# Clustered attention and a two-of-eight expert layer on one core: v's scales on ScalarE, stores and third list later, other staging for pairs 13 and 14

## The chip, the core and the metric

The kernel runs as one launch on one core of a Trainium2 chip. The metric is the device time in microseconds (us), lower is better. TensorE (PE; PEld is its weight load), VectorE (DVE), ScalarE (ACT) and GpSimd (POOL) compute, and SyncE (SP) issues most DMAs. Each engine works through its own queue in the order in which the kernel's text issued the instructions; between engines only semaphores count.

## The reference

Attention over 4 batches, 8 heads, 768 positions, head size 64; a query sees only keys whose nearest centroid (of 16) is its own. Its output, 3072 rows of 512, goes through an expert layer in which each row uses its two best of 8 experts.

```python
mask = q_assign[:, :, :, None] == k_assign[:, :, None, :]
scores = np.where(mask, scale * q @ k.T, -1e9)
x = softmax(scores) @ v                       # 3072 rows of 512
noisy = x @ w_gate + log1p(exp(x @ w_noise)) * noise
top2 = argpartition(-noisy, 2)[:, :2];  w = softmax(noisy[top2])
out[rows of e] += w * (relu(x @ w1[e]) @ w2[e])     # e = 0 .. 7
```

## The kernel before

**Attention.** Heads go in 16 pairs (4 pairs a batch). The loop over steps `t` runs 12 steps a pair: each step makes the scores of one head's 128 keys against 768 queries (`scores`, line 531), their exponential on ScalarE (line 532, tile `pe`), the lower half of that exponential (`split_p`, line 543, tile `pl`: the f32 value less its upper 16 bits) and, four steps later, the products with v (`values`, lines 560 to 566). The lower halves run on GpSimd up to step 173, and on VectorE from step 174 (pair 14's sixth block) on.

Everything else is hung into this loop by a table `sched`: `at(step, f, ...)` puts a call into one of three slots of a step (thirds). `w = 12 * (p - 2)` is a pair's base, `z` is `w + 40` of a batch's last pair, or 192 in the lines behind the loop over pairs. The number is only a place in the text, not a time: an engine does its instructions in that order, as soon as what they wait for is there. Of the calls that matter here:

- `x_am` (line 611), once for each half batch: four numbers a partition, v's scales times the batch's power of two (`px`), a `tensor_scalar` on VectorE, at step 48b+7.
- `x_hi` (ACT, line 629), `x_lo` (GpSimd, line 633) and `x_put` (a DMA on SP, line 639): a pair's output as two f16 halves, stored to `xs` in DRAM. A pair goes in two pieces, i = 0 and 1. Pairs 1 to 12 use one tile `xh`, and one store. Pairs 13 and 14 use two tiles each of the pool `xg`, which has four buffers and which the gathers of the experts use too. Pair 15 is done after the attention.
- `a_mask`, `b_mask`: a pair's cluster mask, built and put by four DMAs (tile `mk`) into the operand `A`, 3.3 steps ahead of its maxima (`b_max`).
- `g_gate`, `g_list`: batch by batch the gate is computed on VectorE, and each row's place and weight are scattered into the table `tbl` by 12 indirect DMAs on GpSimd (line 821), each behind a small memset (line 820). The third batch's gate ends in a part that starts with `places` (matmuls, line 733). Batch 3 has no scatter: its list is made by matmuls inside the expert part.
- `load_w1`, `load_w2`: the first expert's weights, eight loads of 512 KB into the tile `stg` (seven buffers); `max_w1`, `max_w2` and `split_w1`, `split_w2` take their largest value and their two f16 halves.
- `load_list(0)` (line 840) reads the first expert's first four columns of the table once all 36 scatters have landed; `gather_x(0, t)`, t = 0 to 3 (lines 1172, 1173), clears an `xg` tile on GpSimd and gathers 128 rows of `xs` into it.

**Experts.** `turn_x` turns a gathered tile by a transposing DMA on SP (line 1184); `layer1` (line 1193) needs all four for its first block, and the halves of w1 from `split_w1`. `layer1` of expert 0 interleaves with batch 3's gate. From `layer2(0, 0)` on (line 1230), expert follows expert.

Of the kernel before, what the change touches and what calls it, by code (L numbers as in the profile page):

```python
# [9 lines left out]
F32 = mybir.dt.float32  # L10
F32R = mybir.dt.float32r
BF = mybir.dt.bfloat16
F16 = mybir.dt.float16
I32 = mybir.dt.int32
AF = mybir.ActivationFunctionType
OP = mybir.AluOpType
# [28 lines left out]
class Kernel:  # L45
# [136 lines left out]
    def attention(self, ctx):  # L182
        nc, tc = self.nc, self.tc
        B, H, S, D, NJ = self.B, self.H, self.S, self.D, self.NJ
# [9 lines left out]
        NP = B * H // 2  # L194
# [6 lines left out]
        def at(step, f, *a):  # L201
            sched.setdefault(divmod(round(3 * step), 3), []).append((f, a))

        def chain(step, by, fs):
            for i, f in enumerate(fs):
                at(step + by * i, f)


        T = AT
        for p in range(NP):  # L210
            b, hp = divmod(p, H // 2)
            w = 12 * (p - 2)
            if hp == 0:
                for g in range(2):
                    at(w + T["qk"] + 24 * g + (T["qf"] if (b, g) == (0, 1) else 0), self.load_qk, b, g)
                    v = w + 24 * g
                    V = T["fv"][g] if p == 0 else T
                    at(v + V["v"], self.load_v, b, g)
                    for h in range(0, 4, 2):
                        at(v + V["vscale"] + V["amstep"] * h, self.v_max, b, g, h)  # L220
                    chain(v + V["am"], V["amstep"], self.v_scale(b, g))
                    for h in range(4):
                        at(v + V["vsplit"] + V["vstep"] * h, self.v_split, b, g, h)
            if p == 0:
                at(17.333, self.x_first)
            for i in range(2):
                if p == 0:
                    hi, lo = 18.667 + 1.333 * i, 20.0 + 1.333 * i
                elif p <= NP - 4:
                    hi, lo = w + 34.667 + 6 * i, w + 36 + 6 * i  # L230
                else:
                    hi, lo = w + 40.667 + 0.333 * i, w + 41.333 + 0.333 * i
                if p < NP - 1:
                    at(hi, self.x_hi, p, i)
                    at(lo, self.x_lo, p, i)
                    if p > NP - 4 or i:
                        at(lo + 1, self.x_put, p, i)
            P = T["first"] if p == 0 else T
            w += (0, T["sec"], T["thr"])[p] if p < 3 else 0
            for i in range(4):  # L240
                at(w + P["split"][i], self.a_split, p, i // 2, i % 2)
            if p == 0:
                at(w + P["sims"][0], self.c_turn)
            at(w + P["place"] + (T["place1"] if p == 1 else 0), self.b_place, p)
            for s in range(2):
                at(w + P["sims"][s], self.a_sims, p, s)
            for s in range(2):
                at(w + P["sum"][s], self.a_sum, p, s)
            for k, f in (("max1", self.a_max1), ("ge", self.a_ge), ("ky", self.a_ky), ("max2", self.a_max2),
                         ("eq", self.a_eq), ("mask", self.a_mask), ("bmask", self.b_mask)):  # L250
                at(w + P[k], f, p)
            if p == 0:
                for s in range(2):
                    for j in range(NJ):
                        at(w + P["bmax"][s] + P["bstep"][s] * j, self.b_max, p, s, j)
                    at(w + P["neg"][s], self.b_neg, p, s, 1)
                    at(w + P["negT"][s], self.b_negT, p, s, 1)
            else:
                w = 12 * (p - 2)
                bm, bs = (T["bmax1"], T["bstep1"]) if p == 1 else (T["bmax"], T["bstep"])  # L260
                for s in range(2):
                    for j in range(NJ):
                        at(w + bm + bs * (6 * s + j), self.b_max, p, s, j)
                at(w + T["neg"], self.b_neg, p, 0, 2)
                at(w + T["negT"], self.b_negT, p, 0, 2)
            if hp == H // 2 - 1:
                z = w + 36 + L
                if b + 1 == B:
                    continue
                for jj in range(NJ):  # L270
                    at(z + T["log"] + T["logstep"] * jj, self.g_logits, b, jj)
                    at(z + T["log2"] + T["logstep"] * jj, self.g_logits2, b, jj)
                at(z + T["turn"], self.g_turn, b)
                fs = self.g_gate(b)
                k = b == B - 2
                chain(z + T["gate"], T["gstep"] / (1 + k), fs[:self.GP])
                chain(z + (12.333 if k else T["gplace"]), T["gstep"] / (1 + k), fs[self.GP:])
                for j in range(2 * NJ):
                    at(z + (15.333 + 2 * min(j, 5) + max(j - 5, 0) if k else T["list"] + T["lstep"][b] * j), self.g_list, b, j)
        at(T["zlist"], self.zero_list)  # L280
        at(-13, self.exp_table)
        at(10.667, self.load_gate)
# [2 lines left out]
        z = 12 * NP  # L285
# [8 lines left out]
        for i in range(4):  # L294
            at(z - 24 + i, self.load_w1, 0, i)
            at(z - 13 + 2 * i, self.max_w1, 0, i)
            at(z - 4 + 2 * i, self.split_w1, 0, i)
            at(z - 8 + i if i < 3 else z - 2, self.load_w2, 0, i)
        at(z - 11.667, self.load_list, 0)
        for i in range(self.TA):  # L300
            at(z - 5.333 + 0.333 * i, self.gather_x, 0, i)
        for i in range(2):
            nc.gpsimd.memset(self.oh[i], 0.0)
        nc.gpsimd.memset(self.nm.bitcast(F32), 0.0)
# [4 lines left out]
        for t in range(min(sched)[0], z + L + 2):  # L309
# [8 lines left out]
            if 0 <= u < z:  # L318
                p, s, kc = u // 12, (u % 12) // 6, u % 6
# [288 lines left out]

    def x_am(self, b, g):
        am = self.am[b, g]  # L610
        self.nc.vector.tensor_scalar(am[:, 0, :], am[:, 2, :], self.px[:, b:b + 1], None, op0=OP.mult)

    def x_piece(self, p, i):
        b, c = divmod(p, self.H // 2)
        if p <= self.NP - 4:
            cs = slice(64 * i, 64 * i + 64)
            return self.xt[b][:, :, 128 * c + 64 * i:128 * c + 64 * i + 64], self.xh[:, :, 0, cs], self.xh[:, :, 1, cs]
        return self.xt[b][:, 3 * i:3 * i + 3, 128 * c:128 * c + 128], self.xh[i][:, :, 0], self.xh[i][:, :, 1]

    def x_hi(self, p, i):  # L620
        NJ = self.NJ
        if p > self.NP - 4:
            pool, n, k = (self.mo, "xh", 2) if p == self.NP - 1 else (self.mw, "xg", 4)
            t = pool.tile([128, 2 * self.DM], F16, name=n, bufs=k)
            self.xh = (self.xh if i else []) + [t[:, :NJ * 128].rearrange("p (j i c) -> p j i c", i=2, c=128)]
        elif i == 0:
            self.xh = self.pre.tile([128, NJ, 2, 128], F16, name="xh")
        x, hi, lo = self.x_piece(p, i)
        self.nc.scalar.activation(hi, x, AF.Copy)
# [5 lines left out]
    def x_put(self, p, i):  # L635
        b, c = divmod(p, self.H // 2)
        NJ, W = self.NJ, 2 * self.DM
        j, n, h = (3 * i, 3, self.xh[i]) if p > self.NP - 4 else (0, NJ, self.xh)
        self.nc.sync.dma_start(rap(self.xs, (b * 128 * NJ + j) * W + 256 * c, [[NJ * W, 128], [W, n], [1, 256]]),
                               h.rearrange("p j i c -> p j (i c)"))  # L640

# [213 lines left out]
    def experts(self, ctx):  # L855
        nc, tc, E, DM, F, N, CAP, T, TA = self.nc, self.tc, self.E, self.DM, self.F, self.N, self.CAP, self.T, self.TA
        ND, NF, NJ, b = DM // 128, F // 128, self.NJ, self.B - 1
# [10 lines left out]
        Bs = (TA * 128, CAP)  # L868
        for t in range(TA):
            self.turn_x(0, t)  # L870
        self.load_list(1)
        for c in range(4):
            self.max_w2(0, c)
        self.layer1(0, 0, [A])
        for j in range(NJ):
            self.g_logits(b, j)
            if j:
                self.g_logits2(b, j - 1)
        self.g_logits2(b, NJ - 1)
        for f in (self.x_hi, self.x_lo, self.x_put):  # L880
            for i in range(2):
                f(self.NP - 1, i)
        self.g_turn(b)
        fs = self.g_gate(b)
        cut = [0] + AT["cut"] + [self.GP, len(fs)]
# [277 lines left out]
    def split_w2(self, e, c):  # L1163
        self.scaled_halves(self.w2t[:, :, 2 * c:2 * c + 2], self.stg[2, c], self.sw2)

    def gather_x(self, e, t):
        xg = self.mw.tile([128, 2 * self.DM], F16, name="xg", bufs=4)
        r = self.rows(t)
        first = e == 0 and t < self.TA
        n = self.N - self.S if first else self.N  # L1170
        if first:
            self.nc.gpsimd.memset(xg, 0.0)
        self.nc.gpsimd.indirect_dma_start(  # L1173
            out=xg[:r], out_offset=None, in_=self.xs[:n],
            in_offset=bass.IndirectOffsetOnAxis(ap=self.entry(e, t)[:r], axis=0),
            bounds_check=n - 1, oob_is_err=False)
        self.xg[e, t] = xg
# [113 lines left out]
```

## Time and profile before

| | |
|---|---|
| time, median of 3 runs | 1084.91 us (1084.48 to 1087.84) |
| profiled execution: time, span | 1085.09 us, 1083.3 us |
| busy in the span: PE, DVE, POOL, ACT | 1008.4, 684.4, 577.5, 513.5 us |
| chain that ended last, by engine | PE 65%, POOL 11%, issue 9%, DVE 8%, DMA 3%, ACT 2% |
| attention's last product ends, first `layer1` starts | 499.3 us, 504.7 us |

The time lies 1.8 us above the span. A busy share over the whole span mixes the attention (to 500 us), where four engines work side by side, with the experts, where PE is busy throughout. So the stretches are read one by one; steps and us are related by about 2.3 us a step, 1.7 us in steps 163 to 173.

### The profile page before, as it was taken

The numbers are of one execution on the slowest core, as the hardware profiler recorded it, in microseconds if no ns is written. First come the engines' busy times: TensorE is split into PE (matmuls) and PEld (weight loads), VectorE is DVE, ScalarE is ACT, GpSimd is POOL, SyncE is SP. The second block draws the span as 40 slices with busy tenths as digits, with TensorE's granted clock in tenths as the row PEclk, the third lists the DMA queues.
The fourth block names the chain that finished last, engine by engine and source line by source line (L and its number), as shares of the span: only waits on it lengthen the run. The fifth ranks groups of instructions, "written<-read, shape, count | busy, mean of one in ns | idle before, by whom it ended". The sixth has DMA issues, their size and how long they took to land.

```text
span 1083.3 us, 22212 instructions
## 1 busy us (share of the span) xinstructions
PE 1008.4 (93%) x8518; PEld 686.4 (63%) x8518; DVE 684.4 (63%) x1451; ACT 513.5 (47%) x1067; POOL 577.5 (53%) x630
## 2 busy tenths in 40 slices
PE   5789999999899999986999999999999999999994
PEld 4678898889788887874455545545455454554542
DVE  5788677887778777896736644456544555455511
ACT  2467676768676767654513523316233152331510
POOL 9167685789877896872243525225252252432211
PEclk8799999999999999998999999999999999999997
DMA  7676766676757754325088853928739278292200
GB/s 195 166 186 148 179 166 173 160 189 160 189 140 175 178 129 107 122 90 100 15 219 172 218 160 102 226 90 186 180 95 240 86 167 199 89 234 84 59 33 33
DMA packets 154113, 158.09 MB, mean 146 GB/s; under 512 B 68970, under 2 KB 132842, under 8 KB 154003
## 3 DMA queue, kind: packets, MB, share of 16 engines
q1 hardware_dynamic: 140706, 120.25, 46.0%
q0 software_dynamic: 13296, 36.38, 11.9%
q8 instruction: 68, 1.11, 0.4%
q14 instruction: 43, 0.34, 0.1%
HBM read 78.21 MB, written 26.51 MB: 97 GB/s over the span
## 4 chain that ended last, share of the span: by engine, by line
PE 65%; POOL 11%; issue 9%; DVE 8%; DMA 3%; ACT 2%; SPq 0%; POOLq 0%; DVEq 0%; ACTq 0%
PE ring L1193 21%; PE ring L1230 20%; PE ring L531 7%; POOL pl L543 4%; PE ring L500 4%; PE av L560 2%; PE av L566 2%; PE av L562 2%; DVE aux L503 1%; DMA A<-mk 1%; PE ring L398 1%; POOL tbl L821 1%; PE ring L419 1%; PE ring L434 1%; ACT pe L532 1%
## 5 line engine op out<-in xcount | busy, mean ns | idle before, releaser
L543 POOL TENSOR_TENSOR pl<-pe 128x768 f16<-128x768 f32 x173 | 251.7, 1469 | 65.9 <-ACT pe L532 61.8
L1193 PE MATMUL ring<-xT,w1t 128*128 128x416 f16 (+2 forms) x1536 | 275.3, 341 | 5.8 <-DMA xT<-xg 5.8
L1230 PE MATMUL ring<-w2t,hT 128*128 128x512 f16 x1152 | 251.8, 379 | 0.0
L532 ACT ACTIVATE pe<-ring,l 128x384 f32<-128x384 f32 x384 | 201.2, 578 | 65.7 <-PE ring L531 60.1
L1193 PEld LDWEIGHTS <-w1t 128*128 128x128 f16 x1536 | 149.9, 98 | 125.5 <-DMA xT<-xg 6.2
L1077 ACT ACTIVATE hr<-ring 128x416 f32<-128x416 f32 (+2 forms) x128 | 66.7, 521 | 289.3 <-PE ring L1193 289.3
L1230 PEld LDWEIGHTS <-hT 128*128 128x128 f16 x1152 | 112.3, 98 | 133.1
L1243 POOL DMA_INDIRECT out<-yo,idx x52 | 62.6, 1204 | 227.7 <-DVE yo L1239 113.6
L503 DVE TENSOR_REDUCE aux<-ring 128x1 f32<-128x384 f32 x192 | 107.9, 562 | 75.3 <-PE ring L500 70.9
L531 PE MATMUL ring<-A 128*128 128x384 f32 x384 | 143.0, 372 | 1.7 <-DVE aux L503 1.0
L531 PE MATMUL ring<-B 128*128 128x384 f32 x384 | 131.3, 342 | 1.6 <-DMA B<-nt 1.6
L500 PE MATMUL ring<-A 128*128 128x384 f32 x384 | 110.6, 364 | 14.6 <-DMA A<-mk 6.2
L1080 DVE TENSOR_TENSOR hT<-hr,hT 128x416 f16<-128x416 f32 (+3 forms) x128 | 71.2, 559 | 82.0 <-ACT hT L1079 81.7
L1239 DVE SCALAR_TENSOR_TENSOR yo<-ring,we,xt 128x512 f32<-128x512 f32 (+1 forms) x49 | 36.7, 749 | 123.4 <-PE ring L1230 104.0
L503 DVE TENSOR_REDUCE mm<-ring 128x1 f32<-128x384 f32 x192 | 104.9, 547 | 0.0
L1173 POOL DMA_INDIRECT xg<-xs,idx x52 | 56.0, 1077 | 80.8 <-DMA xT<-xg 69.5
L560 PE MATMUL av<-vv,pe 128*128 128x65 f16 x1152 | 97.5, 195 | 1.4 <-DVE xt L574 1.4
L562 PE MATMUL av<-vv,pe 128*128 128x64 f16 x1152 | 96.5, 192 | 0.0
L560 PEld LDWEIGHTS <-pe 128*128 128x128 bf16 x1152 | 79.7, 99 | 16.7 <-issue 11.9
L500 PEld LDWEIGHTS ring<-A 128*128 128x128 f32 x384 | 71.0, 195 | 27.4 <-ACT pe L532 12.1
L562 PEld LDWEIGHTS <-pe 128*128 128x128 bf16 x1152 | 78.1, 98 | 0.3
L531 PEld LDWEIGHTS ring<-A 128*128 128x128 f32 x384 | 74.0, 193 | 3.0 <-DVE aux L503 1.2
(210 smaller groups left out, 1437.9 us busy)
## 6 DMA issues: line engine op xcount, KB each, us to landing
stg<-in_moe_w SPq DMA_DIRECT2D x64, 512.0 KB
A<-hl SPq DMA_DIRECT2D x30, 384.0 KB
B<-hl SPq DMA_DIRECT2D x30, 384.0 KB
vt<-in_v SPq DMA_DIRECT2D x8, 768.0 KB
out<-zt SPq DMA_DIRECT2D x12, 512.0 KB
A<-hl SPq DMA_DIRECT2D x60, 96.0 KB
B<-hl SPq DMA_DIRECT2D x30, 192.0 KB
qk<-in_q SPq DMA_DIRECT2D x7, 768.0 KB
```

The costliest lines, as they stand in the source:

```text
L500: nc.tensor.matmul(t, A[:, 0, s, j * 128:j * 128 + 128], A[:, 1, s, n * 384:n * 384 + 384], start=True, stop=True)
L503: nc.vector.tensor_reduce(o, t, axis=X, op=OP.max, negate=True)
L531: nc.tensor.matmul(t, M[:, 1 - qi, s, ks], M[:, qi, s, ns], start=not qi, stop=bool(qi))
L532: nc.scalar.activation(pe[:, n], t, AF.Exp, bias=self.l64[:, 0:1], scale=self.scale)
L543: (nc.vector if last else nc.gpsimd).tensor_tensor(lo, pe, hi, op=OP.subtract)
L560: nc.tensor.matmul(av[:, j, :], ph[:, js], vv[:, hh, kj, 64:129], start=(kc == 0 and j == 0), stop=False, skip_group_check=True)
L562: nc.tensor.matmul(av[:, j, :64], ph[:, js], vv[:, hh, kj, 0:64], start=False, stop=False, skip_group_check=True)
L1077: nc.scalar.activation(r[:, :n], p, AF.Relu, scale=2.0 ** -HT)
L1080: nc.vector.tensor_tensor(h1, r[:, a:b], h0, op=OP.subtract)
L1193: nc.tensor.matmul(p, self.w1t[:, wi, c, f * 128:f * 128 + 128], self.xT[e][:, c, xi, n0:n1], start=(i == 0), stop=(i == 3 * ND - 1))
L1230: nc.tensor.matmul(p, self.hT[:, hi, f, t * 128:t * 128 + 128], self.w2t[:, wi, f], start=(i == 0), stop=(i == 3 * NF - 1))
L1243: i = nc.gpsimd.indirect_dma_start(out=self.out, out_offset=bass.IndirectOffsetOnAxis(ap=en[:r], axis=0), in_=yo[:r], in_offset=None, boun ...
```

## The change

The products for v's scales go from VectorE to ScalarE. The first piece of x's halves of pairs 1 to 12 is split 3.3 steps later, and the store's call stands at `w + 45` in place of `w + 43`. The end of the third batch's gate starts 1.33 steps later; of its twelve scatters three stand at steps 165.3, 167.7 and 170 (before: six at 163.3 to 173.3, two steps apart, then one a step), the rest at 173 to 175.7. Pair 13's halves use a tile of `stg` and one store; pair 14's two tiles are taken at step 180.67 (`x_tiles`). The clearing of a gather's tile is a call of its own (`clear_x`); tiles 0 and 1 are cleared at steps 181 and 182 and gathered at 182.67 and 183, ahead of pair 14's halves (184.67 to 186.67), tiles 2 and 3 behind its stores. The last two loads of w2 stand behind the four `turn_x`, and their maxima behind pair 15's stores.

```diff
                 elif p <= NP - 4:
-                    hi, lo = w + 34.667 + 6 * i, w + 36 + 6 * i
+                    hi, lo = w + 38 + 2.667 * i, w + 39.333 + 2.667 * i
...
-                    if p > NP - 4 or i:
-                        at(lo + 1, self.x_put, p, i)
+                    if p == NP - 2 or i:
+                        at(w + 45 if 0 < p <= NP - 4 else lo + 1, self.x_put, p, i)
...
-                chain(z + (12.333 if k else T["gplace"]), T["gstep"] / (1 + k), fs[self.GP:])
+                chain(z + (13.667 if k else T["gplace"]), T["gstep"] / (1 + k), fs[self.GP:])
                 for j in range(2 * NJ):
-                    at(z + (15.333 + 2 * min(j, 5) + max(j - 5, 0) if k else ...), self.g_list, b, j)
+                    at(z + ((17.333 + 2.333 * j if j < 3 else 24 + 0.333 * j) if k else ...), self.g_list, b, j)
...
-            at(z - 8 + i if i < 3 else z - 2, self.load_w2, 0, i)
+            if i < 2:
+                at(z - 8 + i, self.load_w2, 0, i)
         at(z - 11.667, self.load_list, 0)
+        at(z - 11.333, self.x_tiles, NP - 2)
         for i in range(self.TA):
-            at(z - 5.333 + 0.333 * i, self.gather_x, 0, i)
+            at(z - 11 + i if i < 2 else z - 6 + 0.333 * i, self.clear_x, i)
+            at(z - 9.333 + 0.333 * i if i < 2 else z - 5.667 + 0.333 * i, self.gather_x, 0, i)
...
     def x_am(self, b, g):
         am = self.am[b, g]
-        self.nc.vector.tensor_scalar(am[:, 0, :], am[:, 2, :], self.px[:, b:b + 1], None, op0=OP.mult)
+        self.nc.scalar.activation(am[:, 0, :], am[:, 2, :], AF.Copy, scale=self.px[:, b:b + 1])
...
+    def x_tiles(self, p):
+        pool, n, k = (self.mo, "xh", 2) if p == self.NP - 1 else (self.mw, "xg", 4)
+        self.xh = [pool.tile([128, 2 * self.DM], F16, name=n, bufs=k)[:, :self.NJ * 128].rearrange(...) for i in range(2)]
...
     def x_hi(self, p, i):
-        if p > self.NP - 4:
-            pool, n, k = (self.mo, "xh", 2) if p == self.NP - 1 else (self.mw, "xg", 4)
-            t = pool.tile([128, 2 * self.DM], F16, name=n, bufs=k)
-            self.xh = (self.xh if i else []) + [...]
-        elif i == 0:
+        if p == self.NP - 3 and i == 0:
+            t = self.mw.tile([128, self.F], F32, name="stg", bufs=7)
+            self.xh = t[:, :NJ * 128].bitcast(F16).rearrange("p (j i c) -> p j i c", i=2, c=128)
+        elif p < self.NP - 3 and i == 0:
             self.xh = self.pre.tile([128, NJ, 2, 128], F16, name="xh")
...
         for t in range(TA):
             self.turn_x(0, t)
+        self.load_w2(0, 2)
+        self.load_w2(0, 3)
         self.load_list(1)
-        for c in range(4):
+        for c in range(2):
             self.max_w2(0, c)
...
+        self.x_tiles(self.NP - 1)
         for f in (self.x_hi, self.x_lo, self.x_put):
             for i in range(2):
                 f(self.NP - 1, i)
+        for c in range(2, 4):
+            self.max_w2(0, c)
...
+    def clear_x(self, t):
+        self.xg[t] = xg = self.mw.tile([128, 2 * self.DM], F16, name="xg", bufs=4)
+        self.nc.gpsimd.memset(xg, 0.0)
```

## Rows read from the trace of the kernel before

**Rows 1.** Busy time (instructions) by stretch, granted clock, DMA share, GB/s:
```profile
core 0: us, PE busy (x) PEld busy (x) DVE busy (x) ACT busy (x) POOL busy (x), PEclk, DMA share, GB/s
443.00:461.00 18.00, 18.00 (x263) 16.56 (x261) 14.24 (x38) 12.60 (x26) 16.45 (x19) 1.00 0.45 148
461.00:475.00 14.00, 10.00 (x114) 8.56 (x113) 13.83 (x19) 6.66 (x13) 12.94 (x15) 0.88 0.11 31
475.00:500.00 25.00, 20.48 (x367) 17.98 (x364) 23.58 (x35) 17.29 (x31) 14.15 (x15) 1.00 0.64 165
500.00:510.00 10.00, 5.34 (x17) 2.31 (x18) 5.55 (x9) 0.32 (x1) 0.00 (x0) 0.66 0.50 60
...
541.00:1070.00 529.00, 527.19 (x2762) 266.64 (x2760) 267.07 (x442) 166.73 (x361) 189.71 (x262) 1.00 0.58 147
```

**Rows 2.** TensorE's timeline: start, length, instruction, [idle before <-who ended it]:
```profile
92.30 0.51 PE L464 MATMUL ring<-identb,oh 128*128 128x128 bf16 x6 [0.98 <-DVE oh L455]
...
295.66 0.55 PE L398 MATMUL ring<-ident,qk 128*128 128x128 f32 x3 [1.55 <-DVE aux L503]
...
410.36 0.55 PE L398 MATMUL ring<-ident,qk 128*128 128x128 f32 x3 [1.58 <-DVE aux L503]
...
435.67 0.21 PE L733 MATMUL aux<-goh,ltri 128*128 128x48 bf16 x2 [1.59 <-DVE goh L726]
...
471.57 0.39 PE L517 MATMUL ring<-ident,nm 128*128 128x128 f32 x1 [3.03 <-DVE nm L512]
...
504.66 4.99 PE L1193 MATMUL ring<-xT,w1t 128*128 128x512 f16 x12 [5.34 <-DMA xT<-xg]
```

**Rows 3.** Line 611, v's scales: durations ns min/median/max, first and last start:
```profile
L611 DVE TENSOR_SCALAR am<-am,px x8: 215/816/4495, 90.1 to 409.6; 128x4 f32<-128x4 f32 x8
```

**Rows 4.** Timelines of VectorE and of GpSimd around the third batch's scales:
```profile
290.52 4.62 DVE L611 TENSOR_SCALAR am<-am,px 128x4 f32<-128x4 f32 x2
...
290.67 4.31 POOL L543 TENSOR_TENSOR pl<-pe 128x768 f16<-128x768 f32 x3
```

**Rows 5.** Line 767, a small ScalarE product scaled by the same power:
```profile
L767 ACT ACTIVATE rec<-aux,px x4: 270/271/273, 226.2 to 530.3; 128x6 f32<-128x6 f32 x4
```

**Rows 6.** SP's timeline, a mask and the store behind it:
```profile
120.28 3.41 SPq L472 DMA_DIRECT2D A<-mk  x4
123.79 0.58 SPq L639 DMA_DIRECT2D xs<-xh  x1
```

**Rows 7.** Timelines of VectorE and GpSimd where the lower halves change engine:
```profile
462.60 3.76 DVE L543 TENSOR_TENSOR pl<-pe 128x768 f16<-128x768 f32 x1
...
467.22 2.65 DVE L543 TENSOR_TENSOR pl<-pe 128x768 f16<-128x768 f32 x1
...
462.64 2.89 POOL L543 TENSOR_TENSOR pl<-pe 128x768 f16<-128x768 f32 x2
...
467.25 1.79 POOL L633 TENSOR_TENSOR xg<-xt,xg 128x384 f16<-128x384 f32 x2
```

**Rows 8.** Line 821, the last seven scatters: durations ns, first and last start:
```profile
L821 POOL DMA_INDIRECT tbl<-rec,pk x7: 954/1446/1689, 465.7 to 477.3; - x7
```

**Rows 9.** Timelines of SP, GpSimd and VectorE between the scatters and layer 1:
```profile
479.41 0.34 SPq L840 DMA_DIRECT2D lst<-tbl  x1
...
483.55 1.87 POOL L633 TENSOR_TENSOR xg<-xt,xg 128x384 f16<-128x384 f32 x2 [5.29 <-ACT xg L629]
...
498.82 1.28 DVE L1084 SCALAR_TENSOR_TENSOR w1t<-stg,sw,w1t 128x1024 f16<-128x1024 f32 x1
```

**Rows 10.** Line 1173, the first four gathers: durations ns, first and last start:
```profile
L1173 POOL DMA_INDIRECT xg<-xs,lst x4: 1001/1416/1838, 486.6 to 494.1; - x4
```

**Rows 11.** The chain that ended last: start, length, what; a store and the seam:
```profile
291.99 2.94 DMA xs<-xh
...
494.14 6.09 DMA xg<-xs,lst
500.25 4.36 DMA xT<-xg
```

More of the change, by code (lines that the diff above doesn't have):

```diff
@@ L276, in attention @@
                 chain(z + T["gate"], T["gstep"] / (1 + k), fs[:self.GP])
-                chain(z + (12.333 if k else T["gplace"]), T["gstep"] / (1 + k), fs[self.GP:])
+                chain(z + (13.667 if k else T["gplace"]), T["gstep"] / (1 + k), fs[self.GP:])
                 for j in range(2 * NJ):
-                    at(z + (15.333 + 2 * min(j, 5) + max(j - 5, 0) if k else T["list"] + T["lstep"][b] * j), self.g_list, b, j)
+                    at(z + ((17.333 + 2.333 * j if j < 3 else 24 + 0.333 * j) if k else T["list"] + T["lstep"][b] * j), self.g_list, b, j)
         at(T["zlist"], self.zero_list)
@@ L610, in x_am @@
         am = self.am[b, g]
-        self.nc.vector.tensor_scalar(am[:, 0, :], am[:, 2, :], self.px[:, b:b + 1], None, op0=OP.mult)
+        self.nc.scalar.activation(am[:, 0, :], am[:, 2, :], AF.Copy, scale=self.px[:, b:b + 1])
     def x_piece(self, p, i):
         b, c = divmod(p, self.H // 2)
-        if p <= self.NP - 4:
+        if p <= self.NP - 3:
             cs = slice(64 * i, 64 * i + 64)
@@ L618, in x_piece @@
         return self.xt[b][:, 3 * i:3 * i + 3, 128 * c:128 * c + 128], self.xh[i][:, :, 0], self.xh[i][:, :, 1]
+    def x_tiles(self, p):
+        pool, n, k = (self.mo, "xh", 2) if p == self.NP - 1 else (self.mw, "xg", 4)
+        self.xh = [pool.tile([128, 2 * self.DM], F16, name=n, bufs=k)[:, :self.NJ * 128].rearrange("p (j i c) -> p j i c", i=2, c=128)
+                   for i in range(2)]
     def x_hi(self, p, i):
         NJ = self.NJ
-        if p > self.NP - 4:
-            pool, n, k = (self.mo, "xh", 2) if p == self.NP - 1 else (self.mw, "xg", 4)
-            t = pool.tile([128, 2 * self.DM], F16, name=n, bufs=k)
-            self.xh = (self.xh if i else []) + [t[:, :NJ * 128].rearrange("p (j i c) -> p j i c", i=2, c=128)]
-        elif i == 0:
+        if p == self.NP - 3 and i == 0:
+            t = self.mw.tile([128, self.F], F32, name="stg", bufs=7)
+            self.xh = t[:, :NJ * 128].bitcast(F16).rearrange("p (j i c) -> p j i c", i=2, c=128)
+        elif p < self.NP - 3 and i == 0:
             self.xh = self.pre.tile([128, NJ, 2, 128], F16, name="xh")
@@ L637, in x_put @@
         NJ, W = self.NJ, 2 * self.DM
-        j, n, h = (3 * i, 3, self.xh[i]) if p > self.NP - 4 else (0, NJ, self.xh)
+        j, n, h = (3 * i, 3, self.xh[i]) if p > self.NP - 3 else (0, NJ, self.xh)
         self.nc.sync.dma_start(rap(self.xs, (b * 128 * NJ + j) * W + 256 * c, [[NJ * W, 128], [W, n], [1, 256]]),
@@ L1164, in split_w2 @@
         self.scaled_halves(self.w2t[:, :, 2 * c:2 * c + 2], self.stg[2, c], self.sw2)
+    def clear_x(self, t):
+        self.xg[t] = xg = self.mw.tile([128, 2 * self.DM], F16, name="xg", bufs=4)
+        self.nc.gpsimd.memset(xg, 0.0)
     def gather_x(self, e, t):
-        xg = self.mw.tile([128, 2 * self.DM], F16, name="xg", bufs=4)
         r = self.rows(t)
@@ L1170, in gather_x @@
         n = self.N - self.S if first else self.N
-        if first:
-            self.nc.gpsimd.memset(xg, 0.0)
+        xg = self.xg.pop(t) if first else self.mw.tile([128, 2 * self.DM], F16, name="xg", bufs=4)
         self.nc.gpsimd.indirect_dma_start(
```

## The prediction

> **What bounds the kernel now.** I read the busy time by stretch first, then every stop of TensorE, then the queues around each stop, last the chain that ended last. From 541 us on TensorE is busy for 527.19 of 529.00 us at full clock [rows 1]: no edit touches that part, so a gain must come ahead of it and be handed through unchanged. In 443 to 461 us PE is busy for all 18.00 us, GpSimd for 16.45 of them and in fact never free, since the scatters' small gaps make up the rest. In 461 to 475 us it turns over: VectorE 13.83 of 14.00 us, PE 10.00; and VectorE stays the full one to 500 us (23.58 of 25.00). The seam, 500 to 510 us, has PE at 5.34 us and a granted clock of 0.66 [rows 1]. So a PE stop in the attention is worth its length where PE has no other slack, and is worth nothing between 461 and 500 us unless the seam behind it moves as well.
>
> The stops that the change can reach are six [rows 2]: 0.98 us at 92.3, 1.55 at 295.7, 1.58 at 410.4, 1.59 at 435.7, 3.03 at 471.6 and 5.34 ahead of the first layer 1 at 504.66. Together 14.1 us: the ceiling of the whole change, but for the clock.
>
> I count in the profiled execution's own time: 1085.09 us, a span of 1083.3 and 1.8 around it. It lies 0.2 us above the median of 1084.91.
>
> **v's scales on ScalarE.** Eight VectorE instructions on four numbers take 215 ns at best, 816 in the median and 4495 at worst [rows 3]. The worst is explained by its neighbour: two of them occupy 290.52 to 295.14 us, while GpSimd does three lower halves without a break from 290.67 to 294.98 [rows 4]. VectorE waits for the whole run of GpSimd and is done 0.16 us behind it. At 295.66 PE stops 1.55 us for the maxima queued behind, and the twin at 410.36 stops 1.58 (the last of the eight starts at 409.6) [rows 2, 3]. On ScalarE neither can wait for that, so both stops go: 3.1 us. The first batch's pair, at 90.1 [rows 3], lies 2 us ahead of the 0.98 us stop; ScalarE is nearly as late there, I take half: 0.5. The second batch's has no stop behind it. What is added: eight ScalarE products of 4 numbers. The nearest is one of 6 numbers with the same scale, 0.27 us [rows 5]: eight are 2.2 us if all stood on the path, 0 if all fall into ScalarE's own waits. ScalarE is busy for 12.60 of 18.00 us even in PE's densest stretch [rows 1], and what is queued behind them are exponentials of the next step with six buffers ahead; I take 0. Sum 3.6 us (1.4 to 4.1).
>
> A rule speaks against the 3.1 us. The Trainium skill, SBUF — State Buffer, "Who interferes with whom", says that VectorE and GpSimd share a pair of ports, and that whoever issues first holds it "for the whole instruction". By that rule the wait would end with the one GpSimd instruction in flight, the two stops would have another cause, and 3.1 us of the sum would be 0. Here the wait lasted through three in a row [rows 4], and the measured row decides.
>
> **x's halves and stores.** Nothing is added: the same two upper halves, two lower halves and one store a pair. The store's place moves from 43 to 45 of a pair's base, the next pair's mask stands at 42, and SP has no call between 43 and 45. In the old order already the mask's four DMAs are issued at 120.28 and the store right behind them, at 123.79 [rows 6]; the order on SP's queue is the same after, and the store goes out when its last lower half is done, whose place (step 42) is unchanged. I count 0, and bound it by half an upper half a pair on either side, 11 x 0.2 us: ±2.
>
> **The end of the third gate.** `places` holds PE for 1.59 us at 435.67 because the gate's VectorE chain isn't there yet [rows 2]. 1.33 steps later (over 2 us) it is. But VectorE is itself late there, and the next thing that PE wants of it is the mask's one-hot; that comes earlier only by the few small gate operations that now stand behind it. I take 1.0 of 1.59 (0 to 1.59).
>
> **Lower halves and scatters.** From step 174 VectorE makes lower halves and meets GpSimd's. The one at 462.60 takes 3.76 us, ending 0.83 behind two of GpSimd's (462.64 + 2.89), the one at 467.22 takes 2.65, ending 0.83 behind two `x_lo` (467.25 + 1.79) [rows 7]: 2.9 and 1.8 us lost on the engine that bounds this stretch. A scatter's distance here is (477.3 + 0.95 - 465.7 - 1.79) / 7 = 1.54 us [rows 7, 8]. The new order has four scatters instead of five ahead of GpSimd's last lower half, so that half ends some 1.5 us earlier, 464.0 in place of 465.5; and each `x_lo` of pair 13 now has a scatter beside it, so VectorE waits for one at most. VectorE gains 1.5 + about 1.3 = 2.8 us, and pair 15 starts that much earlier. The stop at 471.57 goes with it. Alone this is worth nothing: it ends the attention at 496.5 instead of 499.3 and makes the seam's wait longer.
>
> **The seam.** Its old chain: pair 14's lower halves at 483.55, for which GpSimd idles 5.29 us [rows 9]; then four times clear and gather, 2.5 us each, the fourth at 494.14 [rows 10, 11]; 6.09 us to land, 4.36 us to be turned, layer 1 at 504.66. The new order puts two of the four into that idle time. In old time: eight scatters and two `x_lo` behind 464.0 end at 464.0 + 8 x 1.54 + 1.8 = 478.1, as late as before (478.2). The list's read was issued 2.1 us behind the last scatter's start (479.41, 477.3) [rows 8, 9]. For its landing no row stands: between the 0.3 us of its issue and the 2.94 of a store [rows 9, 11]; I take 2. Two gathers then start at 481.2 and end at 484.6 (1.42 each [rows 10], 0.3 between). Pair 14's lower halves, 1.9 us, are now queued behind them and end at 486.5, 1.1 later than before, and with them the store's first part leaves at 485.6 and lands by 488.5 at the latest (2.94). Only then may the third tile be cleared: gathers three and four start at 489.6 and 492.1. That is 2.0 us ahead of 494.14. Two turns are then already under way or done and two of w2's loads no longer lie between, for which I add 1 (0 to 3). Layer 1 starts 3.0 us earlier, at 501.7 (0 to 7.4 us). The upper end is w1: its last half is done at 498.82 + 1.28 = 500.10, less VectorE's 2.8: 497.3.
>
> The last two loads of w2 and their maxima move to where VectorE is free (5.55 of 10.00 us [rows 1]); layer 2 wants them tens of us later: 0.
>
> **Sum.** 3.6 + 1.0 + 3.0 = 7.6 us: 1085.1 - 7.6 = 1077.5, and by the median 1077.3. PE still idles some 5 us at the seam, so I leave the lower clock there as it is.
>
> **Rivals.**
> 1. *The seam stays.* The new queue order makes pair 14's lower halves wait for the list, and the two late gathers come out where the old four did. For it: 486.5 above is later than the old end; against: two of the four are out of the way. Gain 3.6 + 1.0 = 4.6: 1080.5. Chance 0.15.
> 2. *The scales don't wait for GpSimd's run*: something else held VectorE, and holds its next instruction in their place. Then 0.5 + 1.0 + 3.0 = 4.5 us are left: 1080.6. The 0.16 us between the two ends speaks against it. Chance 0.07. (This is what the Trainium skill's rule of SBUF — State Buffer, above, comes to here.)
> 3. *The seam opens fully.* Stores land faster than 2.94 us, the early turns leave the queue empty, layer 1 starts at 497.3, and PE's wait is too short for the clock to fall. 7.4 us, and of the 5.34 us worked at 0.66 some 1.7: 1085.1 - 3.6 - 1.0 - 7.4 - 1.7 = 1071.4. Chance 0.13.
> 4. *Slower: the list's landing becomes the bound of the seam.* Place: GpSimd's queue, where gathers 0 and 1 now stand ahead of pair 14's lower halves, its stores and gathers 2 and 3. Each us by which the last scatter ends behind 478.1 goes to layer 1. It decides from 478.1 + 3.0 + 4.6 = 485.7, which is 2.5 us a scatter; the longest instruction of the seven took 1.689 us [rows 8] next to VectorE's lower halves, and now eight, not seven, share that stretch with them. At 2.9 us a scatter the list is 10.9 late: 1077.5 + 10.9 = 1088.4. Chance 0.07.
> 5. *Nothing is kept.* The stops that go come back at the next wait for VectorE, and the seam's tile order costs what it saves: 1084.5. Chance 0.08.
>
> **How the numbers follow.** The forecast has 0.50, its own range 1074 to 1080.5 (scales 1.4 to 4.1, gate 0 to 1.6, seam 1 to 5). Changes within 0.3%, 3.3 us, can't be told from none here: 1081.7 to 1088.2. Faster: the forecast, rivals 3, and most of 1 and 2, which lie 1.1 us inside: 0.80. Same: 5, the rest of 1 and 2, part of 4: 0.14. Slower: 0.06. The range 1071 to 1083 leaves out rivals 4 and 5 and the tail of 3, 0.18.
>
> **What would show it.** Line 611 on ACT at about 0.25 us, no PE stop over 1 us between 285 and 300 or 400 and 415. No VectorE lower half over 2.5 us behind step 174. The first gather ahead of pair 14's `x_lo`, two more behind its stores, the fourth some 2 to 3 us ahead of where it stood, by the time elapsed since step 174. Layer 1 first at 501.7 - 4.6 = 497 us in the new trace, and from there to the end the same 578.6 us as before (1083.3 - 504.7). Wrong if the mask's or the operand `B`'s DMAs wait behind the store, if the stops at 295 and 410 persist, or if the span behind layer 1 has grown.

## The result and the profile after

| | before | changed |
|---|---|---|
| time, median of 6 runs each on one chip | 1085.01 us (1083.15 to 1087.84) | 1076.75 us (1073.96 to 1079.14) |
| ratio, 95% interval | | 0.992 (0.990 to 0.994) |
| profiled execution: time, span | 1085.09, 1083.3 us | 1074.16, 1072.4 us |
| first `layer1` starts | 504.7 us | 494.5 us |

The forecast was 1077.3 us. The profiled execution of the changed kernel lies 2.6 us below its own median, so its trace shows more gain than the change brings: 1.4 us are already there at the first edited step, and some 1.6 come from a stretch near 130 us that ran at a granted clock of 0.89 before and at 1.00 here (a repeat of the same kernel, below, has 0.89 there too). To keep that out, I count the seam's times from the first lower half that VectorE makes: 460.80 us before, 452.47 after.

Busy time by stretch, the columns as in [rows 1]; the three early stretches are those of [rows 1] some 8 to 10 us earlier:

```profile
453.00:465.00 12.00, 9.83 (x132) 8.56 (x131) 11.83 (x19) 6.64 (x13) 11.06 (x13) 0.86 0.13 36
465.00:490.00 25.00, 20.79 (x346) 18.55 (x343) 23.77 (x35) 17.15 (x30) 15.42 (x17) 0.93 0.42 115
490.00:500.00 10.00, 5.60 (x26) 2.60 (x26) 4.27 (x7) 1.08 (x3) 0.00 (x0) 0.83 0.68 184
530.00:1060.00 530.00, 527.44 (x2764) 266.68 (x2761) 266.63 (x442) 166.96 (x361) 190.06 (x263) 1.00 0.60 147
```

VectorE is still the full engine from 453 to 490 us and the experts still keep PE busy throughout. What the stops of TensorE became, in its timeline:

```profile
99.38 0.63 PE L503 MATMUL ring<-A 128*128 128x384 f32 x2 [0.97 <-DMA A<-mk]
...
289.70 0.49 PE L401 MATMUL ring<-ident,qk 128*128 128x128 f32 x3
...
402.02 0.49 PE L401 MATMUL ring<-ident,qk 128*128 128x128 f32 x3
...
430.82 0.21 PE L740 MATMUL aux<-goh,ltri 128*128 128x48 bf16 x2 [1.29 <-DVE aux L506]
...
461.19 0.45 PE L520 MATMUL ring<-ident,nm 128*128 128x128 f32 x1 [2.17 <-DVE nm L515]
...
484.89 0.24 PE L563 MATMUL av<-vv,pe 128*128 128x65 f16 x1 [2.44 <-DVE xt L577]
...
494.45 4.44 PE L1207 MATMUL ring<-xT,w1t 128*128 128x512 f16 x12 [4.16 <-DMA xT<-xg]
```

Against [rows 2]: the stop at 295.66 is gone (289.70 is the same instruction, with no idle time in brackets), and its twin at 410.36 too (402.02). The stop of 0.98 us at 92.3 is gone as well, but one of 0.97 us, for a mask's DMAs, stands at 99.38, where there was none. The gate's stop shrank from 1.59 to 1.29 us and has another releaser; 3.03 became 2.17, 5.34 became 4.16, and a stop of 2.44 us stands near the attention's end. The line of v's scales, to be held against [rows 3] (durations in ns: least, median, most):

```profile
L614 ACT ACTIVATE am<-am,px x8: 285/288/293, 86.7 to 400.1; 128x4 f32<-128x4 f32 x8
```

Where the lower halves change engine, VectorE's timeline:

```profile
452.47 1.19 DVE L546 TENSOR_TENSOR pl<-pe 128x768 f16<-128x768 f32 x1 [0.24 <-ACT pe L535]
454.52 2.33 DVE L546 TENSOR_TENSOR pl<-pe 128x768 f16<-128x768 f32 x1
...
457.71 1.78 DVE L546 TENSOR_TENSOR pl<-pe 128x768 f16<-128x768 f32 x1
...
460.96 1.16 DVE L546 TENSOR_TENSOR pl<-pe 128x768 f16<-128x768 f32 x1
...
478.26 2.63 DVE L546 TENSOR_TENSOR pl<-pe 128x768 f16<-128x768 f32 x1
```

The first four take 6.46 us in sum; before they took 8.32 (0.96 and 0.95 beside the 3.76 and 2.65 of [rows 7]). The last row is new: it starts with pair 14's `x_lo`, the third row of GpSimd's timeline:

```profile
475.89 1.04 POOL L1187 DMA_INDIRECT xg<-xs,lst  x1 [3.07 <-DMA lst<-tbl]
477.24 1.00 POOL L1187 DMA_INDIRECT xg<-xs,lst  x1 [0.30 <-issue]
478.26 1.80 POOL L640 TENSOR_TENSOR xg<-xt,xg 128x384 f16<-128x384 f32 x2
483.59 0.95 POOL L1180 MEMSET xg<- 128x1024 f16 x1 [3.53 <-DMA xs<-xg]
484.82 1.01 POOL L1187 DMA_INDIRECT xg<-xs,lst  x1 [0.27 <-POOL xg L1180]
...
487.07 1.63 POOL L1187 DMA_INDIRECT xg<-xs,lst  x1 [0.27 <-POOL xg L1180]
```

The two brackets of over 3 us are the new waits of the seam: for the list, then for pair 14's store. The chain that ended last runs through just these (start, length, what):

```profile
470.00 3.51 DMA tbl<-rec,pk
473.53 1.53 DMA lst<-tbl
...
479.22 4.27 DMA xs<-xg
...
487.07 4.17 DMA xg<-xs,lst
491.26 3.06 DMA xT<-xg
494.45 4.45 PE ring L1207 x12
```

Before, the list and the store that the third tile waits for were not in it. Ahead of the gathers it ran through pair 14's halves on ScalarE and GpSimd (the same view of the kernel before):

```profile
482.94 0.53 ACT xg L629
...
483.55 0.41 POOL xg L633
```

Us from VectorE's first lower half, before and after:

| | before | after |
|---|---|---|
| last scatter starts | 16.5 | 17.5 |
| list's read is issued | 18.6 | 21.1 |
| pair 14's `x_lo` ends | 24.6 | 27.6 |
| fourth gather starts | 33.3 | 34.6 |
| last turn starts | 39.4 | 38.8 |
| layer 1 starts | 43.9 | 42.0 |

### The profile page after: what moved, and what is told of

Read it like the earlier page. It is cut to its first block, busy times and chain, and to the rows that moved or that the text cites. A ratio compares the mean times of both kernels' runs of the same rounds, so it can differ in the third digit from the quotient of the medians.

```text
span 1072.4 us, 22220 instructions
## 1 busy us (share of the span) xinstructions
PE 1004.8 (94%) x8518; PEld 684.0 (64%) x8518; DVE 671.4 (63%) x1443; ACT 513.8 (48%) x1075; POOL 577.3 (54%) x630
## 4 chain that ended last, share of the span: by engine, by line
PE 70%; issue 8%; POOL 7%; DVE 6%; DMA 4%; ACT 2%; SPq 0%; POOLq 0%; DVEq 0%; ACTq 0%
PE ring L1207 22%; PE ring L1244 20%; PE ring L534 9%; PE ring L503 5%; PE av L563 2%; PE av L569 2%; PE av L565 2%; DMA A<-mk 2%; PE ring L422 1%; POOL pl L546 1%; DVE aux L506 1%; PE ring L401 1%; PE ring L437 1%; POOL tbl L828 1%; ACT pe L535 1%
## 5 line engine op out<-in xcount | busy, mean ns | idle before, releaser
L503 PEld LDWEIGHTS ring<-A 128*128 128x128 f32 x384 | 69.4, 190 | 27.6 <-ACT pe L535 13.7
```

The source lines that it names most:

```text
L503: nc.tensor.matmul(t, A[:, 0, s, j * 128:j * 128 + 128], A[:, 1, s, n * 384:n * 384 + 384], start=True, stop=True)
```

## The experiments

Times are medians; the ratio is to the kernel before in runs on the same chip.

**Scales alone, and scales undone.**

```diff
 before.py, line 611
-        self.nc.vector.tensor_scalar(am[:, 0, :], am[:, 2, :], self.px[:, b:b + 1], None, op0=OP.mult)
+        self.nc.scalar.activation(am[:, 0, :], am[:, 2, :], AF.Copy, scale=self.px[:, b:b + 1])
```

> The kernel before with one edit alone: v's scales on ScalarE. Theory (VectorE's product waits for GpSimd's whole run of lower halves): the product takes 0.29 us on ScalarE, the two PE stops of 1.55 and 1.58 us behind the third and fourth batch's scales are gone, part of the one at 92 us too; 3.6 us faster than before (3.0 to 4.5). Rival (something else holds VectorE): the stops stay under another instruction, at most 0.5 us faster.

Measured: 1080.86 against 1086.03 us, ratio 0.9957 (0.9941 to 0.9973): 4.7 us. In its trace both stops are gone. That trace was taken in a run 2.6 us above the median and shows less: it is 4.8 us ahead at VectorE's first lower half, but this one takes 4.40 us in place of 0.96, beside two of GpSimd's, and layer 1 starts only 2.7 us earlier.

The same line of the changed kernel put back on VectorE:

> The changed kernel with v's scales back on VectorE. Theory: the two stops come back, 1.5 us each, and the product takes up to 4.5 us there again; 3.1 to 4.1 us slower than the changed kernel. Rival (the other edits have moved GpSimd's run away from the product, or the path went elsewhere): within 1 us of the changed kernel.

Measured: 1080.66 us, ratio 0.9953 (0.9935 to 0.9971): against 0.992 for the whole change about 3.6 us are lost, against the 0.993 of its repeat (below) 2.5. Its VectorE durations and its stops of PE are those of before again:

```profile
293.93 0.55 PE L401 MATMUL ring<-ident,qk 128*128 128x128 f32 x3 [1.55 <-DVE aux L506]
...
408.15 0.55 PE L401 MATMUL ring<-ident,qk 128*128 128x128 f32 x3 [1.59 <-DVE aux L506]
```

```profile
L614 DVE TENSOR_SCALAR am<-am,px x8: 216/817/4508, 88.5 to 407.4; 128x4 f32<-128x4 f32 x8
```

**Breaks in GpSimd's run.** On the kernel before, a small memset behind each of GpSimd's lower halves around the two long stalls:

```diff
         (nc.vector if last else nc.gpsimd).tensor_tensor(lo, pe, hi, op=OP.subtract)
+        if 98 <= 12 * p + 6 * s + kc < 106 or 146 <= 12 * p + 6 * s + kc < 154:
+            nc.gpsimd.memset(self.spacer, 0.0)
```

> The kernel before with an 88 ns memset on GpSimd (it reads nothing) behind each lower half of steps 98 to 105 and 146 to 153, the product of v's scales still on VectorE. Theory (VectorE waits for an unbroken run of GpSimd instructions that read): the pair of products at the third and fourth batch takes 0.4 to 1.7 us in place of 4.6, and the two stops of PE are gone. Rival (the run of instructions holds VectorE whatever stands between them): 4.6 us and more, as before.

Measured: one run of 1083.83 us beside 1086.46. VectorE's product, and GpSimd beside it:

```profile
287.78 4.63 DVE L613 TENSOR_SCALAR am<-am,px 128x4 f32<-128x4 f32 x2
```

```profile
287.88 1.46 POOL L543 TENSOR_TENSOR pl<-pe 128x768 f16<-128x768 f32 x1
289.28 0.09 POOL L545 MEMSET spacer<- 1x1 f32 x1
289.34 1.46 POOL L543 TENSOR_TENSOR pl<-pe 128x768 f16<-128x768 f32 x1
290.74 0.09 POOL L545 MEMSET spacer<- 1x1 f32 x1
290.80 1.46 POOL L543 TENSOR_TENSOR pl<-pe 128x768 f16<-128x768 f32 x1
```

The breaks let nothing in: VectorE is done at 292.41, 0.15 us behind the third lower half, and PE's stops stayed at 1.58 and 1.73. That the wait ends with GpSimd's run holds; that any other instruction between its lower halves ends it fell. The memsets made no gap, though: each lower half starts before the memset ahead of it ends (289.34 against 289.28 + 0.09). What an idle GpSimd would do is not shown by this run.

**x's stores undone, and alone.**

```diff
 changed kernel
-                    hi, lo = w + 38 + 2.667 * i, w + 39.333 + 2.667 * i
+                    hi, lo = w + 34.667 + 6 * i, w + 36 + 6 * i
...
-                        at(w + 45 if 0 < p <= NP - 4 else lo + 1, self.x_put, p, i)
+                        at(lo + 1, self.x_put, p, i)
```

> The changed kernel with x's halves and stores of pairs 1 to 12 at their old steps. Theory (SP's order is the same, so nothing moves but ScalarE's 3 us wait for the first store at 103 us): 0 to 0.5 us slower than the changed kernel. Rival (the stores' place is what moved the attention by 1.6 us between steps 30 and 39 and by small amounts later): 1.5 to 2.5 us slower.

Measured: 1079.59 us, ratio 0.9945 (0.9927 to 0.9963). That is some 2 us above the whole change (0.992, in the repeat 0.993), as the rival has it, with intervals that overlap. So the part was also tried by itself, these lines turned round on the kernel before:

> The kernel before with the new steps for x's halves and stores of pairs 1 to 12 alone. By the trace with these undone: 0.8 us for ScalarE's wait at 103 us and 0.3 at two or three later places, 1 to 2 us faster than before. Rival (SP's order is the same, nothing moves): within 0.5 us.

Measured: 1085.61 against 1086.46 us, ratio 0.9998 (0.9984 to 1.0012): nothing, as the rival has it. Its one trace reaches step 174 2.6 us early and loses 2.8 right there, where VectorE's first lower half takes 4.36 us. One small gain does come with the new places. Between the exponentials of steps 22 and 23 ScalarE gains 3.4 us on the kernel before, and at step 26 0.6 of it is left. Each of the eight traces with the new places has this, and none of the five others.

**Gate and lists undone, and alone.**

```diff
 changed kernel
-                chain(z + (13.667 if k else T["gplace"]), ...)
+                chain(z + (12.333 if k else T["gplace"]), ...)
...
-                    at(z + ((17.333 + 2.333 * j if j < 3 else 24 + 0.333 * j) if k else ...), self.g_list, b, j)
+                    at(z + (15.333 + 2 * min(j, 5) + max(j - 5, 0) if k else ...), self.g_list, b, j)
```

> The changed kernel with the third gate's end and its scatters at their old steps. Theory from the two traces (the stop at places went from 1.59 to 1.29 us and nothing else came of it; the scatters end as late in both orders): the waits of VectorE's lower halves are back at 3.8 and 2.7 us, the attention ends some 2 us later, layer 1 starts 0 to 1.5 us later; 0 to 1.5 us slower than the changed kernel. Rival (the scatters' order carries the seam): 3 us slower or more.

Measured: 1077.61 us, ratio 0.9925 (0.9909 to 0.9941): the same as with them. The waits of 3.8 and 2.7 us that were expected did not come. VectorE's first four lower halves take 5.57 us in sum, less than in the new order (6.46). Its first one starts at 456.29, ahead of GpSimd's last two, and from there the two engines take turns: VectorE's second waits only for the one of GpSimd's that is under way, and GpSimd's two take 3.67 us in place of 2.89 [rows 7].

```profile
458.10 1.29 DVE L546 TENSOR_TENSOR pl<-pe 128x768 f16<-128x768 f32 x1
...
457.04 3.67 POOL L546 TENSOR_TENSOR pl<-pe 128x768 f16<-128x768 f32 x2
```

Its layer 1 still waits, 5.47 us, and starts 41.1 us behind VectorE's first lower half:

```profile
497.41 4.41 PE L1207 MATMUL ring<-xT,w1t 128*128 128x512 f16 x12 [5.47 <-DMA xT<-xg]
```

The two lines turned round on the kernel before:

> The kernel before with the third gate's end and its scatters at their new steps alone. Theory (the new order trims VectorE's waits behind step 174 by 2 us but lands the list 1 us later, and the seam takes its time from the list): the attention ends 1 to 2 us earlier, PE's wait ahead of layer 1 grows from 5.3 to 6 us or more, within 1.5 us of before. Rival (VectorE's waits are what the seam follows): 2 to 3 us faster.

Measured: 1082.28 against 1083.91 us, ratio 0.9984 (0.9964 to 1.0004), not told from no change. The attention ends some 1.8 us earlier, counted from VectorE's first lower half, and PE's wait ahead of layer 1 grows from 5.34 to 6.49 us:

```profile
501.92 1.46 PE L1193 MATMUL ring<-xT,w1t 128*128 128x512 f16 x3 [6.49 <-DMA xT<-xg]
```

**Staging alone, beside the whole change again.** On the kernel before, only the edits of pairs 13 and 14, of the four clears and gathers and of w2's loads:

```diff
+        at(z - 11.333, self.x_tiles, NP - 2)
         for i in range(self.TA):
-            at(z - 5.333 + 0.333 * i, self.gather_x, 0, i)
+            at(z - 11 + i if i < 2 else z - 6 + 0.333 * i, self.clear_x, i)
+            at(z - 9.333 + 0.333 * i if i < 2 else z - 5.667 + 0.333 * i, self.gather_x, 0, i)
...
```

> The kernel before with the staging edits alone (pair 13 in stg, two gathers early, w2's last loads behind the turns). Theory (the seam gains by itself): layer 1 starts 2 to 3 us earlier than before and the whole is 2 to 3 us faster. Rival (the gathers gain only together with the new scatter order): within 1 us of before. Layer 1's PE wait would be 2 to 3 us in the first case, 5 in the second.

> The changed kernel once more, beside the others: 0.992 of before, 1077 us; its PE wait ahead of layer 1 about 4 us.

Measured: staging alone 1077.19 us, ratio 0.9936 (0.9919 to 0.9953); the whole change 1077.08, ratio 0.993 (0.9913 to 0.9947); before 1083.66. One part is worth as much as all, and more than twice the 2 to 3 us expected. In staging alone PE doesn't wait for a turn at all (VectorE holds the attention's last products, 1.34 us, and layer 1 follows them):

```profile
497.55 0.35 PE L569 MATMUL av<-vv,pl 128*128 128x65 f16 x6 [1.34 <-DVE pl L546]
497.74 2.54 PE L1207 MATMUL ring<-xT,w1t 128*128 128x512 f16 x11
```

In the whole change it waits 5.34 us again (about 4 were expected), first in TensorE's timeline and then in the chain:

```profile
498.65 4.77 PE L1207 MATMUL ring<-xT,w1t 128*128 128x512 f16 x12 [5.34 <-DMA xT<-xg]
```

```profile
474.37 2.95 DMA tbl<-rec,pk
477.34 1.54 DMA lst<-tbl
...
483.21 3.92 DMA xs<-xg
...
491.22 4.24 DMA xg<-xs,lst
495.47 3.04 DMA xT<-xg
```

Layer 1 starts 39.3 us behind VectorE's first lower half in staging alone (458.42), 41.8 in the whole (456.81), 43.9 before. In staging alone TensorE's clock also stays at its upper level there: 1.00 in the ten us from 497, against 0.66 in [rows 1] and in the whole change's repeat. Here is staging alone first, then the repeat, with the columns of [rows 1]:

```profile
497.00:507.00 10.00, 8.26 (x90) 4.83 (x90) 7.75 (x11) 5.85 (x13) 0.00 (x0) 1.00 0.30 84
...
494.00:504.00 10.00, 5.35 (x19) 2.49 (x20) 3.29 (x7) 0.55 (x2) 0.00 (x0) 0.66 0.72 186
```

**Taking the store out of the chain.** Pair 14's halves in a tile of `stg`, so that all four gathers stand ahead of them and need no store of theirs; three loads of w2 go behind the turns:

```diff
 changed kernel
-            at(z - 11 + i if i < 2 else z - 6 + 0.333 * i, self.clear_x, i)
-            at(z - 9.333 + 0.333 * i if i < 2 else z - 5.667 + 0.333 * i, self.gather_x, 0, i)
+            at(z - 11 + 0.333 * i, self.clear_x, i)
+            at(z - 9.333 + 0.333 * i, self.gather_x, 0, i)
...
-        if p == self.NP - 3 and i == 0:
+        if self.NP - 3 <= p <= self.NP - 2 and i == 0:
             t = self.mw.tile([128, self.F], F32, name="stg", bufs=7)
```

> The changed kernel with pair 14's halves in a tile of stg too, so that all four gathers stand ahead of them and wait for no store; w2's second load joins the two behind the turns. Theory (the seam's bound is the pair's store, 3.5 us of GpSimd's wait): the fourth gather starts 5 us earlier, PE's 4.2 us wait ahead of layer 1 falls to about 1 us, whose bound is then w1's last half on VectorE; 3 to 4 us faster than the changed kernel. Rival (turns and gathers hold each other up in the queues): the fourth turn lands as late as now, 0 to 1 us.

Measured: 1074.15 against 1083.66 us, ratio 0.9909 (0.9891 to 0.9928). The wait is down from 5.34 to 1.56 us:

```profile
494.00 5.28 PE L1206 MATMUL ring<-xT,w1t 128*128 128x512 f16 x12 [1.56 <-DMA xT<-xg]
```

Next, pair 14's halves and store go behind the turns as well, and w2's second load back to its place:

```diff
         self.load_list(1)
+        for f, i in ((self.x_hi, 0), (self.x_hi, 1), (self.x_lo, 0), (self.x_lo, 1), (self.x_put, 1)):
+            f(self.NP - 2, i)
```

> As the four early gathers, and pair 14's halves and store behind the attention, ahead of the first layer 1's relu. Theory: VectorE no longer waits 1.8 us for pair 14's lower halves at 478 us and PE's 2.4 us stop behind it shrinks, so that the attention ends 1 to 2 us earlier still; 4 to 6 us faster than the changed kernel in all. Rival (w1's halves or the turns bound layer 1): no faster than the four early gathers alone.

Measured: 1070.98 us, ratio 0.9884 (0.9861 to 0.9908). Layer 1 follows the attention without a wait:

```profile
492.07 0.35 PE L568 MATMUL av<-vv,pl 128*128 128x65 f16 x6 [2.06 <-DVE pl L545]
492.26 4.27 PE L1208 MATMUL ring<-xT,w1t 128*128 128x512 f16 x12
```

Last, the same with the old places of the gate's end and the scatters (the edit of "Gate and lists undone"):

> The kernel with four early gathers and pair 14's halves late, and the third gate's end and its scatters at their old steps. Theory (the new scatter order delays the list by 1 to 2 us from step 174 on, and here nothing waits for the list any more): the same within 1 us, 0.988 of before. Rival (the new scatter order is worth something in VectorE's lower halves): 1.5 to 3 us slower, 0.990 to 0.991.

Measured: 1070.4 against 1086.46 us, ratio 0.9851 (0.9834 to 0.9869), the fastest kernel here. Its interval shares 0.9861 to 0.9869 with that of the kernel above, so the old places are not shown to be better. Its gathers run through:

```profile
477.19 1.18 POOL L1188 DMA_INDIRECT xg<-xs,lst  x1 [0.80 <-POOL xg L1181]
...
481.28 1.00 POOL L1188 DMA_INDIRECT xg<-xs,lst  x1 [0.30 <-issue]
```

The fourth starts 26.1 us behind VectorE's first lower half (455.17), against 34.6 in the changed kernel.

## Why the prediction was right, point by point

**Scales: right, mechanism and size, but for the first batch.** Predicted 3.6 us. In the trace after, each of the stretches from step 102 to 105 and 150 to 153, by ScalarE's exponentials, is 1.8 us shorter: the two stops. The 0.5 us taken for the first batch did not stay. By step 21 0.8 us are gained, and right behind, at 99.38, the stop for the mask's DMAs takes them back. Each of the eight traces with the product on ScalarE has that stop, 0.97 to 1.51 us, none of the six with it on VectorE has it. By the runs it is 4.7 us alone and 3.6 or 2.5 out of the whole. The price on ScalarE was 0.288 us each, none of it seen on the path. Rival 2 is out: the two stops went with the product and came back with it. The wait lasts through three lower halves [rows 4] and even through memsets between them. So the Trainium skill's "for the whole instruction" (SBUF — State Buffer, "Who interferes with whom") doesn't describe this wait: it went on past the instruction in flight, for 4.47 to 4.65 us, at the third and the fourth batch of all six traces with the product on VectorE. It is no rule for all of VectorE's instructions either: with the lists undone, a lower half on VectorE got in behind the one of GpSimd's that was under way.

**Stores: right within its bound of 2 us.** Predicted 0, measured 0.9998 alone. The mask's DMAs still stand ahead of the store, as in [rows 6]. What was put at nothing is 0.6 us in the traces, at steps 22 to 26. Why the run with the stores undone lost some 2 us stays open.

**The gate's end: wrong.** Predicted 1.0 us, found 0.3 at the stop (1.59 to 1.29) and nothing at step 174. The step that failed is "I take 1.0 of 1.59". The releaser tells why: no longer the gate's `goh` but `aux` of line 506, a maximum that stands in VectorE's queue ahead of it. VectorE itself was late, and a place further back in the text moves the wait with it. The prediction named this reason and still took off only a third for it.

**Lower halves and scatters: right that it is worth nothing alone, too large in VectorE's gain.** Predicted 2.8 us of VectorE's time, got 1.9 in the first four (8.32 to 6.46). The stop at 471.57, which was to go with it, stayed at 2.17 us. And the gain hangs on when VectorE arrives: once the scales have moved, the old places do as well (5.57 us with the lists undone). "No lower half over 2.5 us" failed once: the one of 2.63 us beside pair 14's `x_lo`, which the new order puts there; it holds PE 2.44 us at 484.89. In the repeat that lower half takes 0.95 and the stop is 1.21. Of the six traces with this staging three have the meeting (2.63, 2.58 and 1.92 us), so it is chance whether the two queues meet there.

**The seam: 2.0 us against 3.0, and the way to it wrong.** The step that failed is "gathers three and four start at 489.6 and 492.1 ... 2.0 us ahead of 494.14". The fourth started 1.3 us later than before (34.6 against 33.3). Three terms were too small. The list's read came 2.5 us later, not as late as before: the last scatter 1.0 later, its landing 3.5 us in place of 2.1. Pair 14's lower halves, queued behind the list's gathers, ended 3.0 us later, not 1.1. Their store took 4.27 us to land, where 2.94 was called the latest [rows 11]. What made up for it is the term priced at 1 us by guess: with two turns and two loads out of the way the last landing fell from 6.09 to 4.17 us and the last turn from 4.36 to 3.06. That is 3.2 us, less the 1.3. So it was luck that the seam came out within 1 us of its forecast: the early gathers were to bring 2.0 us and lost 1.3, and a guess of 1 stood for 3.2. Whether the turns or the loads did it is not shown apart, but it goes with the staging: this landing took 5.1 to 6.5 us and this turn 3.9 to 4.6 in the five traces with the old staging, 3.4 to 4.3 in the six with the new one, and the turn 3.0 to 3.1 in the five of them where PE waits for it.

**The sum.** In the repeat's trace, which has no luck ahead of the edits, VectorE's first lower half starts 4.0 us earlier (3.6 of it in the two stretches of the scales), layer 1 another 2.0 (the seam), and what follows is 0.4 shorter: 6.4 us of span, against a sum of 7.6. Gate and seam were 2.0 too large, what stands ahead of step 174 and behind layer 1 0.8 too small. The medians of the two comparisons give 8.3 and 6.6 us, on either side of the sum. The lower clock was rightly left as it is. If a granted clock between 0.5 and 1.00 is a mix of TensorE's two levels (1.2 and 2.4 GHz), PE stood at the lower one for an estimated 14 x 0.24 + 10 x 0.68 = 10.2 us by [rows 1], and for 12 x 0.28 + 25 x 0.14 + 10 x 0.34 = 10.3 us by the rows after, now in three places and not two.

**What the sum did not see.** Alone the parts gain 4.7, 0.2, 1.7 and 6.9 us by their ratios, each uncertain by some 2 us, 13.5 in sum; together 7.6 to 8.7. Much of the difference lies in the seam. Staging alone shortens it by 4.6 us (43.9 to 39.3) and is then held by the attention. PE waits 1.34 us and not 5.34, the granted clock is 1.00 and not 0.66, and the first 11 matmuls of layer 1 take 2.54 us, where 12 take 4.77 in the whole change; what follows is 2.5 us shorter than before (576.2 against 578.6). That is the clock term of rival 3.

In the whole change the seam is 2.5 us longer than in staging alone (41.8 against 39.3), because its fourth gather starts 3.4 us later (34.4 against 31.0 us behind VectorE's first lower half). Of that 1.9 us are the list's read (20.5 against 18.6), half of it the later scatter and half its landing. Pair 14's store takes 1.8 us longer from its issue to the third tile's clearing (4.0 against 2.3), and a wait of 0.35 us for ScalarE, which stands ahead of it in staging alone, is gone. This is the mechanism of rival 4 in a mild form: the list, with pair 14's halves and store behind it, did become the bound, at a loss of 2.5 us and not of 11. The scatters' new places are not the whole reason. With the old places layer 1 still starts at 41.1 (lists undone), and with the new ones, but the scales back on VectorE, at 39.8. What goes with the longer seam is the store: the same stretch takes 3.7 to 4.4 us in the four traces of this staging with the scales on ScalarE, 2.3 and 2.6 in the two with them on VectorE. Why is not shown.

That the chain was the bound is shown by taking it apart: without the store the median fell by 2.9 us, without the rest of pair 14 by another 3.2 (1077.08, 1074.15, 1070.98 on one chip).

## What to carry to other kernels

When work is moved ahead of something on a queue, price the whole chain that hangs on the thing it now waits for, each landing with its own slack, and don't take the one store in the trace as the latest. A stop whose releaser is a busy engine does not go by calling later what it waited for; look at what else stands in that engine's queue. And edits to one seam don't add: whichever bound comes next (here the attention's end, then the list) takes what the others give.

## What the hardware showed that was not expected

- VectorE's four-number product took 4.63 us beside three GpSimd lower halves with memsets of 0.09 us between them, as long as without (4.62 [rows 4]). Beside a scatter VectorE got through: its first lower half of the kernel before took 0.96 us beside one. Between two of GpSimd's lower halves it got through in the two kernels with the scales moved, the new staging and the lists' old places (1.29 us each). What in GpSimd's work lets it in is not settled.
- The same scatter takes GpSimd 1.29 to 1.70 us where one of VectorE's lower halves is under way as it starts. It takes 0.95 to 0.99 us where the lower half starts 0.26 us or more behind it, or ends just as it starts. In all 14 traces it goes by which of the two starts first.
- The same landing differs between orders of the same DMAs: the last list scatter 2.1 to 3.5 us, the fourth gather 3.4 to 6.5, the last turn 3.0 to 4.6. What sets it is not shown.
